# Moving one chunk's loads behind the second weight matrix, its value casts behind a later unit, and small casts between engines, in a one-core attention and feed-forward kernel

## The chip, the cores and the metric

The kernel runs on one core of one Trainium2 chip. The metric is the device time of one execution in microseconds (us). The kernel before takes 230.92 us in the median of 3 runs (230.06 to 231.16). A core has TensorE (PE in the profile; its weight loads are PEld), VectorE (DVE), ScalarE (ACT), GpSimd (POOL) and SyncE (SP), each with its own in-order stream of instructions; DMAs are issued from the streams of SP, ACT and POOL.

## The reference

Inputs are q, k, v of shape (4, 8, 768, 64): 4 batches, 8 heads, 768 positions, 64 values each. Heads with `retr` 1 attend to all earlier positions; the others ("streams") see only the first 4 positions and a window of 64. A feed-forward part follows.

```python
scores = scale * np.matmul(q, k.transpose(0, 1, 3, 2))
...
mask = np.where(retr[0, :, 0, 0, None, None], full_mask, stream_mask)
scores = np.where(mask[None, :, :, :], scores, -1000000000.0)
...
a = np.exp(scores)
a = a / (np.sum(a, axis=-1, keepdims=True) + 1e-09)
return np.matmul(a, v).astype(np.float32)
...
h = x @ w_in
g = h * (1.0 / (1.0 + np.exp(-beta * h)))
return (g @ w_out).astype(np.float32)
```

Here `x` is the attention output as 3072 rows of 512; `w_in` is 512 x 2048 and `w_out` 2048 x 512.

## The kernel before, in words

The work is cut into 8 chunks (a batch and one half of its positions: 384 queries) and each chunk into 4 units (a pair of heads, p = 0 to 3): 32 units, unit u in chunk u // 4. Chunks are computed two batches at a time, first halves before second halves, so the "third chunk" is number 2, units 8 to 11, the second half of batch 0.

For a unit of the first three chunks the steps are these. `load_qk` (L123) brings float32 rows of k and q into staging tiles `s0` (pairs 0 and 1) and `s1` (pairs 2 and 3); `load_v` (L143) brings the values into `vs`, in three 256 KB pieces. With `held`, a tiny memset of the tile by another engine stands ahead of the load, so that the load waits for that engine alone. `cast` (L288) makes bfloat16 copies `qkb` of k and q; `cast_dp(u)` puts k's cast on DVE and leaves q's on POOL, `cast(u)` puts both on POOL. `steps_T` (L363) transposes them on PE and copies them into `KT` and the padded query tiles `QTP` (whose other halves `zero_q` sets to zero). `sinks_of` (L344) copies key blocks of streams into `KO`. `steps_QK` (L442) makes scores and exponentials `es`. `values` (L304) casts the values into `VX` (`cast_v`, L298) and makes the stream copies `VO` on POOL. `steps_PV` (L497) multiplies `es` by `VX` and `VO` into `po`; DVE divides by the sums (`rec`, `x`). `steps_X` (L536) transposes `x` into `xT`; for later units a DMA does it. From chunk 3 on, rows go through POOL's cast DMAs (`load_rows`, L322, twelve 64 KB pieces per chunk: six of k, then six of q, into tiles that `rows` (L249) takes from the same staging pools) and DMA transposes instead.

The feed-forward part has two kinds of step: a "first product" `steps_G1` (L569; four matmuls with `w_in_sb`, a tanh on ACT, a gate on DVE into `gT`), 16 per chunk, and a "second product" `steps_G2` (L592; four matmuls with `w_out_sb`, four such steps to one output tile), 12 per chunk. `next_m` chooses the next one and `ms(n)` takes n of them. `w_in` comes by `load_w_in` (L158), `w_out` by `load_w_out` (L164), both cast during the DMA and issued by POOL.

All five engines' streams are in program order: the order of the calls at L725 to L853 (written out by hand) and of the slots behind it is the order on each engine. `later(delay, fn)` puts a small piece off until the estimated clock has gone on by `delay` ns, which places it in the stream some steps further down. From L1015 the strings `SEQ` give the order of the steps of each group of scores: `1` a first product, `2` a second product, `p` half of a unit's PV; `PVS` names the units.

Names of the steps below: unit 8's T, QK and PV are T(8), QK(8), PV(8); "product 5" is the fifth first product. In the profile a first product is PE L579, a second product PE L623, T is PE L371, QK is PE L486, PV is PE L514, X is PE L546, scores of later groups are PE L961; `cast` is L296, `cast_v` L302, the copies of `sinks_of` L354 and L355, of `values` L315 and L316, `zero_q` L260; the loads are L138 (q, k), L152 (v), L162 (w_in), L166 (w_out), L328 (rows); DMA transposes are L339 (keys, queries) and L530 (x).

Of the kernel before, what the change touches and what calls it, by code (L numbers as in the profile page):

```python
# [17 lines left out]
def kernel(  # L18
# [13 lines left out]
    nc = tc.nc  # L32
# [55 lines left out]
    def later(delay, fn):  # L88

        todo = [fn]  # L90

        def once():
            if todo:
                todo.pop()()
        heapq.heappush(heap, (clock[0] + delay, count[0], once))
        count[0] += 1
        return once
# [5 lines left out]
    def step(s):  # L103
        cost, fn = s
        flush(clock[0])
        clock[0] += cost
        fn()
# [15 lines left out]
    def load_qk(c, g, pairs=1, held=False):  # L123

        b, h2 = chunks[c]
        rows = slice(h2 * HALF, (h2 + 1) * HALF)
        both = stage.tile([128, 2, 2, 2, HT, D], F32, name=f"s{g}")
        for i, (name, src) in enumerate((("k", k), ("q", q))):
            staged[name, c, g] = both[:, i]
            if held:  # L130
                nc.gpsimd.memset(staged[name, c, g][:, 0, 0, 0, 0:1], 0.0)
        n = 2 // pairs
        for i in range(pairs):
            for name, src in (("k", k), ("q", q)):
                h = 2 * g + n * i
                eng = nc.scalar if c == 0 and name == "q" else nc.sync
                for hs in [slice(0, 2)] if n == 1 else [slice(0, 1), slice(1, 2)]:
                    eng.dma_start(  # L138
                        out=staged[name, c, g][:, n * i:n * (i + 1), hs].rearrange("p a h t d -> p (a h) (t d)"),
                        in_=src[b].rearrange("(c a) s d -> a c s d", c=2)[h:h + n, hs, rows, :].rearrange(  # L140
                            "a c (p t) d -> p a c (t d)", t=HT)[:, 0 if n == 1 else slice(0, n), slice(0, 2) if n == 1 else 0])

    def load_v(c, held=False, tiles=range(HT)):  # L143
        b, h2 = chunks[c]
        if tiles[0] == 0:
            staged["v", c] = stage.tile([128, HT, H, D], F32, name="vs")
        vs = staged["v", c]
        if held:
            nc.gpsimd.memset(vs[:, :, 0, 0:1], 0.0)
        for t in tiles:  # L150
            r = h2 * HALF + t * 128
            nc.sync.dma_start(out=vs[:, t], in_=v[b, :, r:r + 128, :].rearrange("h p d -> p h d"))  # L152
# [5 lines left out]
    def load_w_in(i, n=1):  # L158
        f = slice(i * 512, (i + n) * 512)
        view = moe_w_in.rearrange("(c a d) f -> c d a f", c=2, a=MO)  # L160
        for c in range(2):
            nc.gpsimd.dma_start(out=w_in_sb[c * D:(c + 1) * D, :, f], in_=view[c][:, :, f])  # L162

    def load_w_out(i):  # L164
        f = slice(i * 4, (i + 1) * 4)
        nc.gpsimd.dma_start(out=w_out_sb[:, f, :], in_=moe_w_out.rearrange("(fo fi) d -> fi fo d", fi=128)[:, f, :])  # L166
        w_done.add(i)
# [90 lines left out]
    def zero_q(i):  # L258
        for hh in range(2):
            nc.vector.memset(QTB[i][hh][half(1 - hh), :], 0.0)  # L260
# [4 lines left out]
            if streams[p]:  # L265
                eng.memset(VO[b, p][:, :, :, D:D + 1], 1.0)

    for i in range(2):
        zero_q(i)
    negatives()  # L270

# [16 lines left out]
    def cast(u, names=("k", "q"), on=None):  # L288
        b, h2, p = units[u]
        c = u // NPAIR  # L290
        s = st_u.setdefault(u, {})
        if "qkb" not in s:
            s["qkb"] = att.tile([128, 2, HT, 2, D], BF16, name="qkb", bufs=4)
        for name in names:
            copy = on or nc.gpsimd.tensor_copy
            copy(out=s["qkb"][:, "qk".index(name)], in_=staged[name, c, p // 2][:, p % 2].rearrange("p h t d -> p t h d"))  # L296

    def cast_v(u):  # L298
        b, h2, p = units[u]
        c = u // NPAIR  # L300
        copy = nc.scalar.copy if u in (2, 3) else nc.vector.tensor_copy if u < 2 or u in (5, 7) or 8 <= u < 16 else nc.gpsimd.tensor_copy
        copy(out=VX[b % 2, p][:, h2 * HT:(h2 + 1) * HT, :, 0:D], in_=staged["v", c][:, :, p:H:NPAIR, :])  # L302

    def values(u):  # L304

        b, h2, p = units[u]
        ka, kz = (1, 2) if h2 == 0 else (2, 5)
        n = kz - ka
        st_u.setdefault(u, {})["values"] = lambda: None
        cast_v(u)  # L310
        if not streams[p]:
            return
        vx, vo = VX[b % 2, p], VO[b % 2, p]
        h0 = streams[p][0]
        nc.gpsimd.tensor_copy(out=vo[:, ka - 1:kz - 1, :, 0:D], in_=vx[:, ka:kz, h0:2, 0:D])  # L315
        nc.gpsimd.tensor_copy(out=vo[0:n_sink_i, ka - 1:kz - 1, :, 0:D],  # L316
                              in_=vx[0:n_sink_i, 0:1, h0:2, 0:D].to_broadcast([n_sink_i, n, 2 - h0, D]))
# [45 lines left out]
    def steps_T(u):  # L363
        b, h2, p = units[u]
        s = st_u.setdefault(u, {})

        def go():
            tk, tq = tile_t(), tile_t()
            for i, tp in ((1, tk), (0, tq)):
                for t in range(HT):  # L370
                    nc.tensor.transpose(tp[:, t, :], s["qkb"][:, i, t].rearrange("p h d -> p (h d)"), ident)  # L371
            copy = nc.scalar.copy if u == 4 else nc.vector.tensor_copy
            copy(out=KT[b % 2, p][:, h2 * HALF:(h2 + 1) * HALF].rearrange("p (j t) -> p j t", t=HT),
                 in_=tk.rearrange("p t j -> p j t"))
            if u in (3, 7):
                sinks_of(u)
            s["QT"] = QT = QTB[u % 3]
            for hh in range(2):
                copy = nc.vector.tensor_copy if hh else nc.scalar.copy
                copy(out=QT[hh][half(hh), :].rearrange("p (j t) -> p j t", t=HT),  # L380
                     in_=tq[half(hh)].rearrange("p t j -> p j t"))

            if u >= 8:
                s["values"] = later(1500, lambda: values(u))
            if u not in (3, 7):
                s["sinks"] = later(600, lambda: sinks_of(u))
        return [(350, go)]

# [147 lines left out]
    def steps_X(u):  # L536
        b, h2, p = units[u]
        s = st_u.setdefault(u, {})

        def go():  # L540
            c = u // NPAIR
            if c not in xT:
                xT[c] = moe.tile([128, MO, HALF], BF16, name="xT", bufs=3)
            tp = tile_t(u)
            for t in range(HT):
                nc.tensor.transpose(tp[:, t, :], s["x"][:, t].rearrange("p h d -> p (h d)"), ident)  # L546
            copy = nc.scalar.copy if u < 8 and u != 3 else nc.vector.tensor_copy
            copy(out=xT[c][:, p, :], in_=tp.rearrange("p t j -> p (t j)"))
            avail.add((c, p))
            since[c] = clock[0]  # L550
            del st_u[u]
        return [(170, go)]
# [90 lines left out]
    first, second = [], []  # L643
# [63 lines left out]
    def transposes_of(u):  # L707
        step(steps_T(u)[0])

    def run(steps):  # L710
        for x in steps:
            step(x)

    def ms(n):
        for _ in range(n):
            step(next_m())
# [3 lines left out]
    def cast_dp(u):  # L720
        cast(u, "k", dve)
        cast(u, "q")
# [12 lines left out]
    special[0] = Banks(2, 3)  # L735
    transposes_of(1)
    special[0] = None
    zero_q(2)
    st_u[0]["sinks"]()
    step(qk[0])  # L740
    step(qk[1])
    step(qk[2])
    cast_dp(2)
    st_u[1]["sinks"]()
    cast(3)
    qk = steps_QK(1)
# [42 lines left out]
    qk = steps_QK(5)  # L789
    step(qk[0])  # L790
    cast(6)
    load_w_in(1)
    cast(7)
    load_w_in(2, 2)
    ms(1)
    step(qk[1])
# [15 lines left out]
    values(6)  # L812
    values(7)
    run(steps_PV(4))
    load_w_out(0)
    load_w_out(1)
    load_qk(2, 0, held=True)
    load_w_out(2)
    load_w_out(3)
    rows("q", "s1")  # L820
    load_v(2)
    load_qk(2, 1)
    ms(1)
    run(steps_PV(5))
    step(steps_X(4)[0])
    ms(1)
    run(steps_PV(6))
    step(steps_X(5)[0])
    ms(1)
    run(steps_PV(7))  # L830
    step(steps_X(6)[0])
    ms(1)
    step(steps_X(7)[0])
    rows("k", "s0")
    rows3 = load_rows(3)
    load_v(3)
    spare[0] = 1
    ms(8)
    for f in masks_late(1):
        f()  # L840
        ms(2)
    ms(8)
    cast_dp(8)
    for i in range(6):
        rows3[i]()
    for i in range(6, 9):
        later(1000 * (i - 3), rows3[i])
    transposes_of(8)
    for m in second[0:4]:
        step(m[1])  # L850
    done[1] += 4
    spare[0] = 0
    ms(2)  # L853
# [140 lines left out]
    def cycle(k, seq, pvs):  # L994
# [7 lines left out]
        for x in seq:  # L1002
# [10 lines left out]
                special[0] = None  # L1013

    SEQ = ["2p2p2", "X2b", "ap1p11p1p11111pp111pp1122", "22c222112112", "p1p11p1p111pp1112pp2", "b12222121212",  # L1015
           "2p1p1112p1p21pp11pp122", "a111c2221212", "212112121212", "pap11p1p112pp112pp22", "221211211112", "211111112112",
           "2p2p22pcp222"]
    PVS = {0: [11], 1: [11], 2: [14, 12, 13, 15], 4: [18, 16, 17, 19], 6: [22, 20, 21, 23], 9: [26, 24, 25, 27], 12: [30, 28]}

# [79 lines left out]
```

## Time and profile before

| | |
|---|---|
| median of 3 runs | 230.92 us |
| the profiled execution | 232.34 us |
| its span, first to last instruction | 230.6 us |
| ACT busy | 156.1 us (68%) |
| DVE busy | 143.4 us (62%) |
| POOL busy | 101.8 us (44%) |
| mean granted TensorE clock | 0.998 |
| bytes moved by DMA | 31.78 MB |

The profile is of one execution. A row of its timeline gives the start and the length in us, the engine, the source line, the operation with output and inputs, the count of instructions merged into the row and, in brackets, how long the engine had been idle before it and what ended that. SPq, POOLq and ACTq are the instruction streams that issue DMAs. Times within the execution are counted from the span's start.

### The profile page before, as it was taken

To read this page: it belongs to the slowest core of one execution; us is meant where nothing else is said; L and a number is where in the kernel's file an instruction comes from. 1 tells how busy PE (TensorE), PEld (TensorE's weight loads), DVE (VectorE), ACT (ScalarE), POOL (GpSimd) and SP (SyncE) were. 2 spreads that over 40 slices of the span, in tenths; PEclk is the share of its full clock that TensorE was granted. 3 is DMA by queue.
4 is the path that set the end of the run, shared out by engine and by line. 5 is a ranking of instruction groups with operands and counts; after the bars stand their busy time and mean duration, and the time that the engine had idled before them with its cause. 6 is when DMAs were issued, how large, how long until landed. Compare 5 with 4: busy or idle time off the path is not lost.

```text
span 230.6 us, 5261 instructions
## 1 busy us (share of the span) xinstructions
PE 219.7 (95%) x1928; PEld 130.3 (57%) x1928; DVE 143.4 (62%) x356; ACT 156.1 (68%) x306; POOL 101.8 (44%) x226
## 2 busy tenths in 40 slices
PE   6889899997999999999999999999999999999994
PEld 2666666653666566545654555454755556556553
DVE  6775879873768589736946593454781676338700
ACT  3899888944667898657874847684938797128621
POOL 6567740454978998057508695840070000000000
PEclk9999999999999999999999999999999999999999
DMA  6999999999999899956998999952832101211012
GB/s 190 258 241 230 148 187 232 206 196 237 200 191 172 122 167 162 139 125 127 167 186 113 105 207 146 149 130 71 179 59 63 45 3 45 82 47 47 3 45 91
DMA packets 95770, 31.78 MB, mean 138 GB/s; under 512 B 82672, under 2 KB 92288, under 8 KB 95744
## 3 DMA queue, kind: packets, MB, share of 16 engines
q1 hardware_dynamic: 58912, 22.33, 47.2%
q0 software_dynamic: 35424, 8.13, 45.6%
q10 hardware_dynamic: 1408, 0.99, 1.4%
q8 instruction: 15, 0.25, 0.5%
q14 instruction: 11, 0.09, 0.1%
HBM read 27.27 MB, written 6.29 MB: 146 GB/s over the span
## 4 chain that ended last, share of the span: by engine, by line
PE 71%; DMA 11%; DVE 5%; ACT 4%; SPq 3%; POOL 2%; issue 1%; ACTq 0%; DVEq 0%; POOLq 0%
PE tp L623 31%; PE mm L579 26%; DMA vs<-in_v_dram 7%; PE po L514 5%; PE sp L961 5%; SPq L152 3%; DMA w_in_sb<-in_moe_w_in_dram 3%; DMA s<-in_q_dram 2%; PE sp L486 2%; ACT es L490 2%; PE tp L606 2%; DVE es L439 1%; DVE x L519 1%; DVE gT L585 1%; PE tp L371 1%
## 5 line engine op out<-in xcount | busy, mean ns | idle before, releaser
L579 PE MATMUL mm<-xT,w_in_sb 128*128 128x384 bf16 x512 | 92.2, 326 | 0.6 <-DMA w_in_sb<-in_moe_w_in_dram 0.4
L623 PE MATMUL tp<-w_out_sb,gT 128*128 128x512 bf16 x368 | 89.3, 379 | 0.0
L582 ACT ACTIVATE th<-mm,beta_h 128x384 f32<-128x384 f32 x128 | 73.1, 598 | 21.3 <-PE mm L579 15.8
L585 DVE SCALAR_TENSOR_TENSOR gT<-th,mm 128x384 bf16<-128x384 f32 x128 | 67.4, 550 | 29.7 <-ACT th L582 25.4
L579 PEld LDWEIGHTS <-w_in_sb 128*128 128x128 bf16 x512 | 48.0, 98 | 32.2 <-issue 1.1
L623 PEld LDWEIGHTS <-gT 128*128 128x128 bf16 x368 | 33.9, 98 | 33.7 <-issue 0.3
L965 ACT ACTIVATE es<-sp 128x512 bf16<-128x512 f32 (+1 forms) x84 | 39.9, 594 | 4.3 <-PE sp L961 4.3
L630 ACT ACTIVATE osb<-tp 128x512 f32<-128x512 f32 x21 | 12.7, 603 | 31.4 <-PE tp L623 29.8
L490 ACT ACTIVATE es<-sp 128x512 bf16<-128x512 f32 (+1 forms) x44 | 22.5, 559 | 5.5 <-PE sp L486 5.1
L514 PEld LDWEIGHTS <-es 128*128 128x128 bf16 x472 | 20.7, 97 | 8.9 <-issue 1.5
L302 POOL CAST VX<-vs 128x384 bf16<-128x384 f32 x18 | 9.3, 526 | 33.0 <-DMA vs<-in_v_dram 30.5
L439 DVE TENSOR_TENSOR es<-es,Mh 128x512 bf16<-128x512 bf16 (+3 forms) x58 | 20.2, 381 | 4.4 <-ACT es L965 3.7
L328 POOL DMA_DIRECT2D s<-in_q_dram x30 | 22.5, 768 | 0.7 <-issue 0.6
L514 PE MATMUL po<-VX,es 128*128 128x65 bf16 x392 | 22.4, 193 | 0.4 <-DVE x L519 0.4
L328 POOL DMA_DIRECT2D s<-in_k_dram x30 | 22.3, 770 | 0.1
L519 DVE TENSOR_TENSOR x<-po,rec 128x384 bf16<-128x384 f32 x32 | 17.8, 558 | 1.1
L486 PE MATMUL sp<-QTP,KT 128*128 128x128 bf16 (+2 forms) x113 | 15.0, 230 | 0.5 <-DVE QTP L380 0.3
L439 DVE TENSOR_TENSOR es<-es,Mc 128x384 bf16<-128x384 bf16 (+2 forms) x21 | 7.8, 370 | 11.4 <-ACT es L965 10.8
L315 POOL COPY VO<-VX 128x128 bf16<-128x128 bf16 (+3 forms) x24 | 9.5, 395 | 10.6 <-DVE VX L302 9.1
L296 POOL CAST qkb<-s 128x384 bf16<-128x384 f32 x15 | 7.5, 520 | 12.5 <-DMA s<-in_q_dram 12.4
L517 DVE RECIPROCAL rec<-po 128x6 f32<-128x6 f32 x32 | 6.1, 190 | 10.7 <-PE po L514 10.7
L354 POOL COPY KO<-KT 128x128 bf16<-128x128 bf16 (+1 forms) x20 | 8.9, 444 | 8.7 <-DMA KT<-s 5.5
(75 smaller groups left out, 166.2 us busy)
## 6 DMA issues: line engine op xcount, KB each, us to landing
vs<-in_v_dram SPq DMA_DIRECT2D x24, 256.0 KB, 5.9
out_dram<-osb SPq DMA_DIRECT2D x23, 256.0 KB, 2.5
s<-in_k_dram SPq DMA_DIRECT2D x12, 192.0 KB, 5.9
w_out_sb<-in_moe_w_out_dram POOLq DMA_DIRECT2D x4, 512.0 KB, 14.7
s<-in_k_dram POOLq DMA_DIRECT2D x30, 64.0 KB, 5.3
s<-in_q_dram POOLq DMA_DIRECT2D x30, 64.0 KB, 5.2
s<-in_q_dram SPq DMA_DIRECT2D x8, 192.0 KB, 6.7
w_in_sb<-in_moe_w_in_dram POOLq DMA_DIRECT2D x4, 256.0 KB, 5.6
```

Of the source, the lines that this page charges most:

```text
L328: nc.gpsimd.dma_start(out=ROWS[c % 2, name][:, t].rearrange("p (a w) -> p a w", a=NPAIR)[:, :, w:w + D], in_=src[b, hh * NPAIR:(hh + 1) * ...
L439: nc.vector.tensor_mul(e, e, m)
L486: nc.tensor.matmul(sp[:, (i - lo) * 128:(j - lo) * 128], lhs, s["QT"][hh][:, q0 * 128:(q0 + j - i) * 128], start=not added, stop=not added ...
L490: nc.scalar.activation(out=es[:, 0:w], in_=sp[:, 0:w], func=ACTF.Exp, scale=scale)
L514: nc.tensor.matmul(po[:, qi, hh, :], e, val, start=(j == 0), stop=(j == len(lst) - 1))
L519: nc.vector.tensor_mul(x, po[:, :, :, 0:D], rec.to_broadcast([128, HT, 2, D]))
L579: nc.tensor.matmul(hp[:, 0:HALF], w_in_sb[:, mo, fi * 128:(fi + 1) * 128], xT[c][:, mo, :], start=(mo == 0), stop=(mo == MO - 1))
L582: nc.scalar.activation(out=th, in_=hp[:, 0:HALF], func=ACTF.Tanh, scale=beta_h[:, fi:fi + 1])
L585: nc.vector.scalar_tensor_tensor(out=gTs[c][:, fi, :], in0=th, scalar=1.0, in1=hp[:, 0:HALF], op0=ALU.add, op1=ALU.mult)
L623: nc.tensor.matmul(op, gTs[c][:, fi, ns * 128:(ns + 1) * 128], w_out_sb[:, fi, :], start=(fi == 0), stop=(fi == FO - 1))
L630: nc.scalar.activation(out=osb, in_=op, func=ACTF.Copy, scale=0.5)
L965: nc.scalar.activation(out=es[:, 0:w], in_=sp[:, 0:w], func=ACTF.Exp, scale=scale)
```

## The change

It has six parts.

1. The three query tiles are all zeroed at the start by DVE; before, two were, and the third after unit 1's transposes.
2. Unit 2's k is cast by POOL instead of DVE. In `cast_v`, unit 2's values are cast by DVE and unit 3's by POOL; ACT did both.
3. Unit 7's casts (POOL) stand ahead of the issue of w_in's second quarter instead of behind it.
4. The loads behind PV(4): before, two issues of w_out, then s0's memset and loads, two issues of w_out, then v(2) and s1. Now s0's memset and loads, four issues of w_out, then s1 with a memset of its own. v(2) is issued later, behind eight more first products and a memset on DVE; v(3) behind unit 8's transposes and four second products, with a memset on DVE as well.
5. First products 5 to 8 are set anew among PV(5) to PV(7) and X(4) to X(7); the row loads of chunk 3 are spread between the second products; unit 8's values are cast behind unit 9's key copies (`sinks_of(9)`, now at once) rather than 1500 ns of estimated clock after unit 8's transposes.
6. In the seventh group's string of `SEQ`, half a PV goes ahead of the first second product and one first product moves up.

```diff
         if held:
-            nc.gpsimd.memset(vs[:, :, 0, 0:1], 0.0)
+            (nc.gpsimd if held is True else held).memset(vs[:, :, 0, 0:1], 0.0)
...
-    for i in range(2):
+    for i in range(3):
         zero_q(i)
...
-        copy = nc.scalar.copy if u in (2, 3) else nc.vector.tensor_copy if u < 2 or u in (5, 7) or 8 <= u < 16 else nc.gpsimd.tensor_copy
+        copy = nc.vector.tensor_copy if u < 3 or u in (5, 7) or 8 <= u < 16 else nc.gpsimd.tensor_copy
...
+            if u == 9:
+                sinks_of(u)
+                values(8)
             if u >= 8:
-                s["values"] = later(1500, lambda: values(u))
-            if u not in (3, 7):
+                s["values"] = later(1500, lambda: values(u)) if u > 8 else lambda: values(u)
+            if u not in (3, 7, 9):
                 s["sinks"] = later(600, lambda: sinks_of(u))
...
-    zero_q(2)
     st_u[0]["sinks"]()
...
-    cast_dp(2)
+    cast(2)
...
     cast(6)
+    cast(7)
     load_w_in(1)
-    cast(7)
     load_w_in(2, 2)
...
     run(steps_PV(4))
-    load_w_out(0)
-    load_w_out(1)
     load_qk(2, 0, held=True)
-    load_w_out(2)
-    load_w_out(3)
+    for i in range(4):
+        load_w_out(i)
+    load_qk(2, 1, held=True)
     rows("q", "s1")
-    load_v(2)
-    load_qk(2, 1)
-    ms(1)
     run(steps_PV(5))
     step(steps_X(4)[0])
+    run(steps_PV(6))
     ms(1)
-    run(steps_PV(6))
     step(steps_X(5)[0])
+    run(steps_PV(7))
     ms(1)
-    run(steps_PV(7))
     step(steps_X(6)[0])
     ms(1)
     step(steps_X(7)[0])
+    ms(1)
     rows("k", "s0")
     rows3 = load_rows(3)
-    load_v(3)
     spare[0] = 1
     ms(8)
+    load_v(2, held=nc.vector)
...
     cast_dp(8)
-    for i in range(6):
-        rows3[i]()
+    transposes_of(8)
+    for i in range(4):
+        step(second[i][1])
+        for j in range(2 * i, min(2 * i + 2, 6)):
+            rows3[j]()
     for i in range(6, 9):
-        later(1000 * (i - 3), rows3[i])
-    transposes_of(8)
-    for m in second[0:4]:
-        step(m[1])
+        later(1000 * (i - 5), rows3[i])
+    load_v(3, held=nc.vector)
...
-           "2p1p1112p1p21pp11pp122", "a111c2221212", "212112121212", "pap11p1p112pp112pp22", "221211211112", "211111112112",
+           "p2p1111p2p121pp11pp122", "a111c2221212", "212112121212", "pap11p1p112pp112pp22", "221211211112", "211111112112",
```

The instructions are the same in number and kind but for the engines named in part 2 and four small memsets ahead of loads, two on DVE and two on POOL. On POOL the order behind PV(4) becomes: s0's memset, w_out four times, s1's memset, q's cast of unit 8, two row loads, KO copies of unit 8, four row loads, q's casts of units 9 and 10, five row loads, VO copies of unit 8, one row load, VO copies of unit 9. On SP v(2) now stands behind s1, and v(3) behind the first output store.

## Prediction

> **What bounds the kernel now.** I read the page's busy times first, then the windows, to see where TensorE is not full.
>
> ```profile
> PE 219.7 (95%) x1928; PEld 130.3 (57%) x1928; DVE 143.4 (62%) x356; ACT 156.1 (68%) x306; POOL 101.8 (44%) x226
> ```
>
> ```profile
> 10.00:20.00 10.00, 8.68 (x129) 6.94 (x127) 7.62 (x21) 9.70 (x23) 5.55 (x25) 1.00 1.17 258
> 20.00:30.00 10.00, 9.38 (x117) 6.97 (x115) 7.21 (x19) 8.61 (x18) 8.40 (x21) 1.00 1.02 152
> 50.00:60.00 10.00, 8.28 (x51) 4.27 (x50) 3.81 (x11) 3.88 (x8) 4.78 (x9) 1.00 1.36 214
> 60.00:200.00 140.00, 139.25 (x1272) 80.77 (x1270) 89.30 (x224) 99.79 (x197) 69.39 (x131) 1.00 1.04 125
> ```
>
> The columns are the window, its length, then PE, PEld, DVE, ACT and POOL busy. PE is the bound: over 140 us behind 60 it lacks 0.75. The holes stand in front: 1.3 us in 10 to 20, where ACT is the full engine (9.70 of 10), 0.6 in 20 to 30, 1.7 in 50 to 60. What is saved there stays saved, since PE behind it is full. The change leaves PE's matmuls as they are, so it can only close holes or open new ones. The chain that ended last says what made them:
>
> ```profile
> 21.30 6.09 DMA w_in_sb<-in_moe_w_in_dram
> ...
> 38.83 15.66 DMA vs<-in_v_dram
> 54.61 0.37 DVE VX L302
> 55.03 0.36 POOL VO L315
> ...
> 55.79 1.43 POOL s L328 x2
> 57.22 0.52 POOL qkb L296
> ```
>
> Ahead of it stand ACT's value casts (their row is in the next part). So there are three: those casts at 14, w_in's second quarter, landed at 27.39, and v(2), landed at 54.49, behind which POOL makes VO(8), two row loads and only then the q cast of unit 9 that T(9) wants.
>
> **Part by part. The start (parts 1 and 2).**
>
> ```profile
> 3.98 0.20 DVE L219 TENSOR_SCALAR Ns<-Md 128x128 bf16<-128x128 bf16 x1 [0.34 <-POOL Md L193]
> 7.92 1.40 POOL L296 CAST qkb<-s 128x384 bf16<-128x384 f32 x3
> 8.40 0.49 DVE L296 CAST qkb<-s 128x384 bf16<-128x384 f32 x1
> 9.49 0.47 ACT L380 COPY QTP<-tp 64x384 bf16<-64x384 bf16 x1 [0.62 <-PE tp L371]
> 13.92 0.92 ACT L302 CAST VX<-vs 128x384 bf16<-128x384 f32 x2
> 13.98 0.29 POOL L316 COPY VO<-VX 4x128 bf16<-4x128 bf16 x1
> 14.73 0.92 ACT L296 CAST qkb<-s 128x384 bf16<-128x384 f32 x2
> 14.89 0.30 POOL L315 COPY VO<-VX 128x128 bf16<-128x128 bf16 x1 [0.62 <-ACT VX L302]
> ```
>
> The third tile's memsets (some 0.5 us) move in front of the masks; DVE waits 0.34 for POOL there, so 0.0 to 0.15 is left: I take 0, and without that wait it would be 0.5. Unit 2's two casts on POOL end at 7.92 + 2 x 0.47 = 8.86, no later than DVE's single one (8.89), but k is ready half a microsecond sooner, so half of T(2)'s 0.5 us lies ahead: ACT's copy starts some 0.2 sooner. ACT then loses its 0.92 of value casts, and unit 4's casts start 1.1 sooner. Not all of it reaches PE: POOL now casts unit 3's values itself (0.5) behind its copies that end at 14.27, so VO(3) starts at 14.27 - 0.2 + 0.5 = 14.57 instead of 14.89. That 0.3, and ACT being free for it, is PE's gain. I take **0.35**; bounds 0 (POOL's five casts cancel it) and 1.1 (ACT's whole time).
>
> POOL's work isn't always equally fast: the cast below took 0.69, where those at 7.92 took 0.47 each.
>
> ```profile
> 62.60 0.69 POOL L296 CAST qkb<-s 128x384 bf16<-128x384 f32 x1
> ```
>
> The slow one ran while DVE multiplied masks. If DVE's value cast of unit 2 held up POOL's VO copies in the same way, by no more than its own length (0.37, as in the chain at 54.61), this part would bring nothing: a rival below. The Trainium skill ("SBUF — State Buffer", section "Who interferes with whom") states such a rule against this part: VectorE's casts in a two-port mode, and its operations with two SBUF inputs, take a port pair that GpSimd shares, and the later of the two blocks. The row above agrees for the mask products; for casts no row here decides.
>
> **Products 5 to 8 (parts 3 and 5).**
>
> ```profile
> 21.91 0.97 POOL L296 CAST qkb<-s 128x384 bf16<-128x384 f32 x2
> 27.35 0.56 DVE L519 TENSOR_TENSOR x<-po,rec 128x384 bf16<-128x384 f32 x1
> 27.52 0.81 PE L579 MATMUL mm<-xT,w_in_sb 128*128 128x384 bf16 x4 [0.44 <-DMA w_in_sb<-in_moe_w_in_dram]
> 31.85 0.17 PEld L546 LDWEIGHTS <-x 128*128 128x128 bf16 x3 [0.48 <-DVE x L519]
> 32.84 0.32 PE L579 MATMUL mm<-xT,w_in_sb 128*128 128x384 bf16 x1 [0.16 <-ACT xT L548]
> ```
>
> Three small stalls: 0.44 for w_in, about 0.3 on X(7), whose weight load had waited 0.48, and 0.16 for the last copy of xT: 0.9. The new order closes the last two: no gates stand between the divisions on DVE, and product 8 covers X(7)'s copy. w_in's issue goes behind 0.97 of casts, against 0.35 gained: it lands 0.6 later, near 28.0. But product 5 comes later too: PE would end PV(4) near 26.7, does PV(5), and X(4) waits for x(4), done at 27.91 - 0.35 = 27.55; X(4) and PV(6) take 0.55, product 5 is at 28.1. So w_in's 0.44 is replaced by 0.45 on x(4), and the other two stay saved: **0.45**. Bounds: -0.5 (w_in lands the full 0.97 later) and 0.9. T(8) comes 0.8 sooner.
>
> **The loads (part 4) and unit 9.**
>
> ```profile
> 43.51 0.50 POOL L296 CAST qkb<-s 128x384 bf16<-128x384 f32 x1 [12.09 <-DMA s<-in_q_dram]
> 48.28 5.34 PE L623 MATMUL tp<-w_out_sb,gT 128*128 128x512 bf16 x24
> 51.65 5.77 SPq L152 DMA_DIRECT2D vs<-in_v_dram  x3
> 56.57 0.55 DVE L296 CAST qkb<-s 128x384 bf16<-128x384 f32 x1 [1.14 <-DMA s<-in_k_dram]
> 57.79 0.34 PE L371 MATMUL tp<-idb,qkb 128*128 128x128 bf16 x3 [1.72 <-POOL qkb L296]
> 61.62 0.28 PE L514 MATMUL po<-VX,es 128*128 128x65 bf16 x4
> ```
>
> The hole at 57.79 is 1.72 of PE. Now neither DVE nor POOL waits for v(2) ahead of unit 9. POOL's order after KO(8) (near 48.1, or 49 as before) is four row loads of 0.75 and q's cast: ready at 52 to 53, while T(9) would come at 55. The hole is closed: **1.7** (0.9 if POOL's row loads take its place, 1.9 at most).
>
> Who is late next? v(2) and s1, 768 KB each, have changed places. s1's k landed at 56.5 (the wait of 56.57), its q by 57.2, where POOL's second cast began; so v(2) lands there at the latest by order alone, and sooner as s0's and s1's loads start earlier. It is wanted by DVE behind KO(9), which is at 59.3 now and near 57 then, and by PV(8), at 61.62 now and 59 then. No wait if it lands by 57; I take **-0.2**, bounds 0 and -3.6, the rival below.
>
> w_out is the other one:
>
> ```profile
> L166 POOL DMA_DIRECT2D w_out_sb<-in_moe_w_out_dram x4: 755/760/770, 28.4 to 30.7; - x4
> ...
> DMA to landing us min/median/max: 9.9/14.7/18.5
> ```
>
> Its last piece lands at 30.65 + 18.5 = 49.15, and the fourth second product, which reads it, stands at 48.28 + 3 x 0.87 = 50.9: 1.75 of cover, 0.95 when PE is 0.8 sooner. s0's loads begin 1.5 us earlier beside it and may take half of the transfers' time then, 0.75; s1 in place of v(2) is not priced by any row. I take **-0.1**, bounds 0 and -0.8.
>
> Behind 60 only one transfer is close:
>
> ```profile
> 64.70 4.01 SPq L339 DMA_TRANSPOSE QTD<-s  x3
> 74.89 0.99 PE L961 MATMUL sp<-QTD,KT 64*128 64x384 bf16 x16
> ```
>
> The query transposes of chunk 3 leave SP by 68.7 and PE wants them at 74.9, at 72.2 after a gain of 2.7. SP's stream ahead of them follows the output stores, thus PE, and chunk 3's row loads end sooner on POOL. I take **-0.1**, bounds 0 and -1.
>
> **The seventh group (part 6).**
>
> ```profile
> 133.77 0.28 PE L514 MATMUL po<-VX,es 128*128 128x65 bf16 x4 [0.21 <-DVE x L519]
> 136.65 0.34 PE L514 MATMUL po<-VX,es 128*128 128x65 bf16 x6 [0.23 <-DVE x L519]
> ```
>
> PE waits twice for a division before it may reuse the `po` bank. In the changed order the first division stands three mask products sooner on DVE (7 of them take 2.55, so 1.1), and PE has a product more in between. The second still stands behind four gates. I take **0.3**, bounds 0 and 0.45.
>
> The sum: 0.35 + 0.45 + 1.7 - 0.2 - 0.1 - 0.1 + 0.3 = 2.4. The profiled execution is 232.34, 1.42 over the median of the runs and 1.74 over its own span; what lies around the span is not touched. 232.34 - 2.4 = 229.94 there, **228.5** in the median.
>
> **The rivals.** *The early gains don't arrive, only T(9)'s does.* POOL is the new queue in front: two casts more, two ahead of w_in. For it: POOL is busy 8.40 of 10 in 20 to 30. Against it: it idles in 10 to 20 (5.55). Then parts 1 to 3 give 0, and 1.7 - 0.4 + 0.3 = 1.6 is left: 229.3.
>
> *POOL is held up beside DVE's cast.* Then the start's 0.35 goes to the 0.37 that unit 2's cast takes on DVE: 228.9. For it speaks the cast of 0.69; against it, that POOL's copies at 13.98 and 14.89 (0.29, 0.30) need only meet DVE's cast once. The rule of the Trainium skill named above ("SBUF — State Buffer") would give this case.
>
> *v(2) becomes the late one, and it is slower.* DVE's stream stops at unit 8's value cast, and behind it stand unit 9's values and unit 8's masks, then PV(8) and all of PE. It decides from the point where v(2) lands later than 57. For it: SP's issues are held back already (v(3)'s three take 5.77), and if v(2) moves only once s1 has landed (57.2), at the pace of those issues (two thirds of 5.77, or all of it), it lands at 61.1 to 63.0. From 61.5, with two casts (0.7) and two masks (an estimate, 0.7 as well), PV(8) comes at 62.9 instead of 61.62: the front's gains are gone and 1.3 is lost, less 0.3 in the seventh group: 231.9. Against it: by bytes it only takes s1's place.
>
> *The hole at T(9) comes back as another wait.* POOL issues six row loads around unit 9's cast, 0.75 each; if KO(8) holds the first four until 51 and s1 is late for unit 10, T(9) or T(10) waits about 1.2: 228.5 + 1.2 = 229.7, no change that can be told.
>
> **How the numbers follow.** Forecast 0.55; T(9) alone 0.17; POOL held up 0.05; the hole comes back 0.11; v(2) late 0.12. A measurement of this kernel can tell about 0.5%, 1.15 us: faster means below 229.77, slower above 232.07. The first three are nearly always below: 0.74. The hole's return, the rest of those three and a fourth of v(2)'s case are within: 0.17. The rest of v(2)'s case is above: 0.09. The best bounds together would take 0.75 + 0.45 + 0.2 + 0.4 + 0.15 = 1.95 more off; they hardly fall together, and I keep 1.7: 226.8. Upward the range covers all cases but most of v(2)'s: 231.2, where v(2) would cost 2.7 more than I take.
>
> **What would show it.** Right: no PE wait on POOL's cast at T(9); ACT's idle 0.62 at 9.49 down to 0.4; unit 4's casts on ACT near 13.7; the wait of 0.44 for w_in gone and one on x(4) in its place; T(8) near 47.2; PV(8) near 59; at 133 one wait of DVE's division fewer. Wrong: DVE idle before unit 8's value cast with v(2) as its releaser, a PE wait on w_out near 50, or a wait on DMA transposes at the first scores of chunk 3. T(8) at 48 would show that the start gave nothing.

## The result and the profile after

The changed kernel takes **229.54 us** in the median of 7 runs (229.31 to 229.70). The kernel before, run beside it, takes 230.66 (7 runs, 230.06 to 232.27). The ratio is 0.994 with a 95% interval of 0.9914 to 0.9966: faster by 0.6%, and 1.0 more than the 228.5 that was forecast. The profiled executions differ by more: 232.34 before, 229.70 after, 2.64. In the sessions below before's median was 230.72 to 230.90 each time, so times of different sessions are set beside each other. A run that the measurement marks as disturbed is left out of the counts and the medians.

The page of the changed kernel, its busy times and the shares of its chain of waits:

```profile
PE 218.5 (96%) x1908; PEld 130.7 (57%) x1928; DVE 143.0 (63%) x358; ACT 155.0 (68%) x304; POOL 102.2 (45%) x230
PE 84%; DVE 6%; ACT 3%; POOL 2%; DMA 2%; issue 2%; SPq 0%; POOLq 0%; ACTq 0%
```

20 matmul records of L626 are missing (348 of 368 on the page), which alone can make PE's busy time look smaller than before's (218.5 beside 219.7). The lines behind L383 have moved by 3: a second product is L626 now, T is still L371. The windows show where the time came from (columns as before: PE, PEld, DVE, ACT, POOL):

```profile
10.00:20.00 10.00, 8.63 (x131) 6.98 (x129) 7.98 (x22) 9.08 (x22) 6.04 (x27) 1.00 1.15 256
20.00:30.00 10.00, 9.25 (x122) 7.00 (x121) 7.51 (x20) 8.10 (x18) 8.16 (x20) 1.00 1.01 167
50.00:60.00 10.00, 9.95 (x72) 5.49 (x72) 5.00 (x16) 5.46 (x11) 8.69 (x15) 1.00 1.64 213
```

The hole in 50 to 60 is gone: PE 8.28 before, 9.95 now. In 10 to 20 ScalarE has lost its value casts (9.70 to 9.08), and PE has gained nothing by it. The timeline of the changed kernel at the places that the prediction named, in order of time (start, duration, then the idle time before it and who ended it):

```profile
5.56 0.51 ACT L296 CAST qkb<-s 128x384 bf16<-128x384 f32 x1 [1.15 <-DMA s<-in_k_dram]
...
9.55 0.47 ACT L380 COPY QTP<-tp 64x384 bf16<-64x384 bf16 x1 [0.60 <-PE tp L371]
...
12.73 0.94 DVE L302 CAST VX<-vs 128x384 bf16<-128x384 f32 x3
13.15 0.29 POOL L315 COPY VO<-VX 128x64 bf16<-128x64 bf16 x1 [0.45 <-DVE VX L302]
13.51 0.24 POOL L316 COPY VO<-VX 4x64 bf16<-4x64 bf16 x1
...
13.98 0.92 ACT L296 CAST qkb<-s 128x384 bf16<-128x384 f32 x2
14.29 0.50 POOL L302 CAST VX<-vs 128x384 bf16<-128x384 f32 x1
14.86 0.30 POOL L315 COPY VO<-VX 128x128 bf16<-128x128 bf16 x1
15.29 0.48 ACT L551 COPY xT<-tp 128x384 bf16<-128x384 bf16 x1 [0.39 <-PE tp L549]
...
26.67 0.30 POOL L315 COPY VO<-VX 128x128 bf16<-128x128 bf16 x1 [1.25 <-DVE VX L302]
27.03 0.46 POOL L316 COPY VO<-VX 4x128 bf16<-4x128 bf16 x1
27.54 0.19 PE L517 MATMUL po<-VO,es 128*128 128x65 bf16 x1 [0.32 <-POOL VO L316]
28.09 0.34 PE L549 MATMUL tp<-idb,x 128*128 128x128 bf16 x3 [0.27 <-DVE x L522]
...
47.64 0.50 PE L371 MATMUL tp<-idb,qkb 128*128 128x128 bf16 x6
47.98 5.34 PE L626 MATMUL tp<-w_out_sb,gT 128*128 128x512 bf16 x23
...
55.43 0.50 PE L371 MATMUL tp<-idb,qkb 128*128 128x128 bf16 x6
...
57.82 0.63 DVE L302 CAST VX<-vs 128x384 bf16<-128x384 f32 x2
59.41 0.28 PE L517 MATMUL po<-VX,es 128*128 128x65 bf16 x4
...
134.01 0.34 PE L517 MATMUL po<-VX,es 128*128 128x65 bf16 x6 [0.17 <-DVE x L522]
```

T(9) at 55.43 waits for nobody, and VectorE's casts of units 8 and 9 at 57.82 find v(2) landed. PV(8) comes at 59.41, near the 59 that was named, and at 133 one of the two waits on a division is gone. In front the signs came late or not at all: T(8) comes at 47.64 and not near 47.2, ScalarE's idle time at 9.55 is 0.60 where 0.4 was forecast, ScalarE's casts for unit 4 start at 13.98, not 13.7 (14.73 before), and VO(3) comes at 14.86, where it came at 14.89: GpSimd's own cast (14.29, 0.50) stands where it used to wait for ScalarE.

One execution each can't price parts of 0.3. The marks below are starts of rows of PE's timeline in all 14 profiled executions of this study: the first scores of unit 4, T(8), the first scores of the group that begins near 77 (L961 with `QTD` and `KT`), and the span.

| kernel | unit 4's scores | T(8) | scores near 77 | span |
|---|---|---|---|---|
| before | 17.56 | 47.95 | 78.97 | 230.6 |
| before again | 17.48 | 47.70 | 79.63 | 231.0 |
| loads alone | 17.50 | 47.96 | 77.08 | 228.4 |
| loads alone again | 17.57 | 48.06 | 77.19 | 228.7 |
| seventh group alone | 17.59 | 47.90 | 77.03 | 228.5 |
| start and products alone | 17.42 | 47.38 | 76.50 | 227.8 |
| changed | 17.51 | 47.64 | 76.76 | 228.0 |
| changed again | 17.16 | 47.12 | 76.25 | 227.1 |
| changed, old start | 17.47 | 47.56 | 76.68 | 227.7 |
| changed, old products | 17.30 | 48.46 | 77.58 | 228.8 |
| changed, old loads | 17.29 | 47.63 | 76.87 | 227.9 |
| changed, old seventh group | 17.36 | 47.71 | 76.83 | 228.2 |
| changed, one more load | 17.29 | 47.29 | 77.57 | 228.4 |
| changed, earlier cast | 17.32 | 48.27 | 77.40 | 228.3 |

### The profile page after: what moved, and what is told of

It reads as the page before. It is cut to its first block, busy times and chain, and to the rows that moved or that the text cites. A ratio compares the mean times of both kernels' runs of the same rounds, so it can differ in the third digit from the quotient of the medians.

```text
span 228.0 us, 5247 instructions
## 1 busy us (share of the span) xinstructions
PE 218.5 (96%) x1908; PEld 130.7 (57%) x1928; DVE 143.0 (63%) x358; ACT 155.0 (68%) x304; POOL 102.2 (45%) x230
## 4 chain that ended last, share of the span: by engine, by line
PE 84%; DVE 6%; ACT 3%; POOL 2%; DMA 2%; issue 2%; SPq 0%; POOLq 0%; ACTq 0%
PE mm L582 34%; PE tp L626 34%; PE po L517 6%; PE sp L961 5%; PE sp L489 2%; DMA s<-in_k_dram 2%; PE tp L609 2%; DVE gT L588 1%; PE tp L371 1%; ACT es L965 1%; DVE QTP L380 1%; DVE es L442 1%; ACT QTP L380 1%; PE tp L549 1%; DVE x L522 1%
## 5 line engine op out<-in xcount | busy, mean ns | idle before, releaser
L626 PE MATMUL tp<-w_out_sb,gT 128*128 128x512 bf16 x348 | 86.7, 379 | 1.1 <-issue 0.2
L626 PEld LDWEIGHTS <-gT 128*128 128x128 bf16 x368 | 33.9, 98 | 33.7 <-issue 0.3
L633 ACT ACTIVATE osb<-tp 128x512 f32<-128x512 f32 x21 | 12.7, 604 | 31.4 <-PE tp L626 29.8
L442 DVE TENSOR_TENSOR es<-es,Mh 128x512 bf16<-128x512 bf16 (+3 forms) x58 | 20.7, 390 | 4.8 <-ACT es L965 4.2
L442 DVE TENSOR_TENSOR es<-es,Mc 128x384 bf16<-128x384 bf16 (+2 forms) x21 | 7.1, 341 | 11.4 <-ACT es L965 10.8
L961 PE MATMUL sp<-QTD,KT 64*128 64x128 bf16 (+2 forms) x199 | 11.8, 232 | 0.0
```

The source lines that it names most:

```text
L442: nc.vector.tensor_mul(e, e, m)
L626: nc.tensor.matmul(op, gTs[c][:, fi, ns * 128:(ns + 1) * 128], w_out_sb[:, fi, :], start=(fi == 0), stop=(fi == FO - 1))
L961: nc.tensor.matmul(sp[:, a * 128:z * 128], lhs[half(h)], st_u[u]["QT"][half(h), q0 * 128:(q0 + z - a) * 128], start=True, stop=True)
```

## The experiments

The theory after the result: the wait at T(9) is a race of v(2)'s landing against VectorE's stream, and it has another length in each execution; the 1.72 of the profiled one was not the usual one. The rival: it is the same in each, and the early parts of the change lost what it gave.

**Before again.** No edit.

> The kernel before, unchanged. Theory: TensorE's wait of 1.72 at T(9) is v(2)'s landing against VectorE's stream, and differs between executions; the profiled execution of before (span 230.6) had a long one, and most have 0.3 to 0.6. Then a second profiled execution has a span near 229 (1.4 less) and a wait at T(9) below 1.0, v(2) landing before 54, with the rest of the program as it was. Rival: the wait is 1.5 to 1.9 in every execution, and the first profiled execution lost its 1.4 elsewhere: then the second one shows the same wait and a difference in front of it or behind it. Timed: the same as before, within 0.3%.

Measured: 230.79 in the median (12 runs, 230.44 to 233.19), ratio to before 0.9992 (0.9961 to 1.0024). The theory expected a short wait in this profiled execution; it was another long one, 232.66. Its timeline:

```profile
55.27 0.36 DVE L302 CAST VX<-vs 128x384 bf16<-128x384 f32 x1 [4.81 <-DMA vs<-in_v_dram]
55.69 0.35 POOL L315 COPY VO<-VX 128x192 bf16<-128x192 bf16 x1 [6.25 <-DVE VX L302]
...
58.44 0.34 PE L371 MATMUL tp<-idb,qkb 128*128 128x128 bf16 x3 [1.96 <-POOL qkb L296]
```

v(2) let VectorE go at 55.27 here and at 54.61 in the first profiled execution: 0.66 later, and the wait is 1.96 beside 1.72, with another one of 0.50 ahead of it for k's cast. So the length goes with the landing in these two. That there are short ones is shown by the next run.

**The seventh group alone.**

```diff
-           "2p1p1112p1p21pp11pp122", ...
+           "p2p1111p2p121pp11pp122", ...
```

> Before with the seventh group's order alone. Theory: 0.4 off (the two traces differ by 0.43 from there on), ratio 0.998; the first of TensorE's two waits on VectorE's division is gone, the second stays near 0.3. Rival: the wait only moves to a later product or PV: ratio 1.000, and TensorE stands where it did at 140.

Measured: 230.23 (7 runs, 229.67 to 231.24), ratio 0.9951 (0.9926 to 0.9976): 0.66 off in the median, more than the theory's 0.4. Its loads are those of before, and this is what its profiled execution (span 228.5) shows at T(9):

```profile
52.20 0.36 DVE L302 CAST VX<-vs 128x384 bf16<-128x384 f32 x1 [1.54 <-DMA vs<-in_v_dram]
...
54.80 0.54 POOL L296 CAST qkb<-s 128x384 bf16<-128x384 f32 x1
55.69 0.50 PE L371 MATMUL tp<-idb,qkb 128*128 128x128 bf16 x6
```

v(2) landed 2.4 to 3.1 sooner than in the two executions above, from loads issued at the same point of the program, and T(9) doesn't wait at all. That settles the theory against its rival: the same loads give a wait of 0, 1.7 or 2 and more. By the landing times in the traces, the last of v(2)'s three pieces lands at 50.9, 51.8 and 52.1 in the three executions with the old loads that don't wait at T(9) (two of them are of kernels further down), and at 54.5 and 55.2 in the two that do.

**Part 4 alone, the loads.** The change's diff from `load_w_out(0)` to `load_v(3)` and in `steps_T`, with the order of X and products of before.

> Before with the loads of chunk 2 (v(2) behind s1, w_out's issues together), unit 8's value cast behind unit 9's copies and the row loads between second products: part 4 alone. Theory: it closes the wait at T(9), which is 0.3 to 0.6 in most runs: 0.4 off the median, ratio 0.998, and the spread of the runs (2.2 us in before) falls below 0.6. Rival, the prediction's term: 1.7 less 0.4 for w_out, v(2) and the transposes, so 1.3 off, ratio 0.9945.

Measured: 230.80 (eleven runs, 230.02 to 233.08), ratio 0.9989 (0.996 to 1.0017): neither the theory's 0.4 nor the forecast's 1.3, and the spread stayed. The profiled execution, one of its quick ones (230.16), has no wait at T(9).

**Part 4 alone, again.** The same kernel once more, for a slower execution.

> Part 4 alone once more, because half of its runs stood 0.7 to 3.5 above its lowest and its one profiled execution was among the quick ones. The changed kernel, with the same loads, had no such run in 19. Theory: its slow runs are executions in which the last piece of w_out lands after 50.9 (49.73 in the quick one, 1.2 of room); a slow profiled execution shows a wait on w_out near 51. Rival: they wait for w_in at 27.5, which the changed kernel's order of products hides behind PV(5) and X(4); then the wait of 0.66 there is longer and nothing waits at 51. Third: v(2) ahead of unit 8's value cast. If the profiled execution is a quick one again, this stays open; the lowest run should then be within 0.2 of before's lowest.

Measured: 230.79 (12 runs, 230.15 to 231.82), ratio 0.9987 (0.9958 to 1.0016). The lowest run is 0.41 above before's (229.74), where 0.2 was expected. The profiled execution was quick again (230.40), without a wait at T(9) or on w_out. What the slower runs of this kernel wait for stays open.

**The start and products 5 to 8 alone**, with the loads and the seventh group of before.

> Before with the start (third zeroed tile at the start, unit 2's and 3's casts as changed), w_in's issue behind both casts and the order of products 5 to 8: the loads and the seventh group stay as before. Theory: the start brings 0, products 5 to 8 bring 0.3 at T(8), and the wait at T(9), which ends with v(2)'s landing, takes that back or most of it: 0 to 0.3 off, ratio 0.999 to 1.000. Rival, the prediction's terms: 0.35 + 0.45 = 0.8 off at T(8), and with the loads issued as much sooner it stays: ratio 0.9965.

Measured: 229.81 (ten runs: nine from 229.25 to 230.48, one at 231.80), ratio 0.9953 (0.9924 to 0.9983): 1.1 off, not the theory's 0 to 0.3; the prediction's 0.8 is nearer. Its T(8) comes at 47.38, and v(2) was early again in the profiled execution, so that nothing was taken back at T(9).

**The changed kernel again**, beside three kernels that differ from it in one thing.

> The changed kernel again, on the chip and beside the runs of before that the other kernels of this call get. Theory: before's runs have a floor near 229.8 and a tail up to 232.9, because TensorE waits at T(9) by as much as the transfers of 30 to 57 us are late in that execution; the change lowers the floor by 0.4 to 0.5 (products 5 to 8) and takes most of the tail away: median 229.6, most runs within 0.5 of the lowest. Rival: the tail only moves to w_out, which in the changed kernel lands 0.75 ahead of the product that reads it (49.86 against 50.6): then part of the runs stand 0.7 to 2 above the lowest, as in part 4 alone, and the median is 230.0 to 230.5.

Measured: 229.39 (12 runs, 228.84 to 229.87), ratio 0.9931 (0.9903 to 0.996), beside 230.72 for before. All 12 lie within 1.03; in 19 runs of the changed kernel there is none that stands apart. The tail is gone, as the theory had it, and the rival's 230.0 or more did not come. The theory's sizes are off: the lowest run is 0.85 below before's (229.69), not 0.4 to 0.5, and only five of the 12 lie within 0.5 of the lowest.

The first of the three has the old start again:

```diff
-    for i in range(3):
+    for i in range(2):
         zero_q(i)
...
-        copy = nc.vector.tensor_copy if u < 3 or u in (5, 7) or 8 <= u < 16 else nc.gpsimd.tensor_copy
+        copy = nc.scalar.copy if u in (2, 3) else nc.vector.tensor_copy if u < 2 or u in (5, 7) or 8 <= u < 16 else nc.gpsimd.tensor_copy
...
+    zero_q(2)
     st_u[0]["sinks"]()
...
-    cast(2)
+    cast_dp(2)
```

> The changed kernel with the start as before (third zeroed tile behind T(1), unit 2's k on VectorE, values of units 2 and 3 on ScalarE). Theory: the start brings nothing, since GpSimd's chain of unit 3's values takes the place of ScalarE's casts: lowest run and median as the changed kernel's within 0.15, T(4) within 0.1 of it. Rival, the prediction's term: 0.35 slower.

Measured: 229.95 (12 runs, 229.38 to 230.67), 0.56 above the changed kernel. So the start is not worth nothing. Its size by the marks: unit 4's first scores come at 17.47 to 17.59 in the six profiled executions with the old start (mean 17.53) and at 17.16 to 17.51 in the seven with the new one that have no other edit in front (mean 17.33): **0.20**. The new start's size hangs on the first loads. ScalarE's cast of unit 1's k is begun when its load lets it; counted from there, unit 4's scores come 12.24 to 12.29 later with the old start and 11.95 to 12.10 with the new one in the same executions, **0.27** apart. Two rows, the first from the changed kernel run again, the others from this one with the old start:

```profile
8.36 0.79 PE L371 MATMUL tp<-idb,qkb 128*128 128x128 bf16 x6 [0.46 <-POOL qkb L296]
```

```profile
8.31 0.49 DVE L296 CAST qkb<-s 128x384 bf16<-128x384 f32 x1
8.85 0.51 PE L371 MATMUL tp<-idb,qkb 128*128 128x128 bf16 x6 [1.00 <-DVE qkb L296]
```

T(2) comes 0.49 sooner, as the prediction had it for k. The changed kernel's first profiled execution, on which "the start gave nothing" rests, is the latest of the seven (17.51); there ScalarE got unit 1's k only at 5.56 (the first row of the timeline above), where in the second it began that cast at 5.15.

The second has the old loads again; unit 8's value cast, the row loads and v(3) go back with them, in hunks not shown:

```diff
     run(steps_PV(4))
+    load_w_out(0)
+    load_w_out(1)
     load_qk(2, 0, held=True)
-    for i in range(4):
-        load_w_out(i)
-    load_qk(2, 1, held=True)
+    load_w_out(2)
+    load_w_out(3)
     rows("q", "s1")
+    load_v(2)
+    load_qk(2, 1)
...
     ms(8)
-    load_v(2, held=nc.vector)
```

> The changed kernel with chunk 2's loads, unit 8's value cast and the row loads as before (so: start, products 5 to 8 and seventh group alone). Theory: the lowest run as the changed kernel's within 0.2, but with before's tail, since T(9) still follows v(2): a third of the runs 0.7 or more above the lowest, median 0.3 to 0.6 above the changed kernel's. Rival: the loads bring nothing at all, and the medians agree within 0.2.

Measured: 229.74 (eleven runs: eight from 229.21 to 230.31, three from 231.79 to 232.51), ratio to before 0.9967 (0.9923 to 1.0011). The lowest run is 0.37 above that of the changed kernel, the median 0.35, and the runs fall in two heaps whose middles are 2.3 apart (229.6 and 231.9), between the 1.9 and 2.8 that T(9) cost in the two executions that waited there (below). The profiled execution was one of the quick ones. With the rest of the change in place, the new loads take the upper heap away; that the upper heap waits at T(9) is the likeliest reading, but it is not shown: no such run was profiled.

The third has one more load, read by nothing, behind w_out's first piece:

```diff
+    more = wpool.tile([128, 2, d_model], BF16, name="more")
     for i in range(4):
         load_w_out(i)
+        if i == 0:
+            nc.gpsimd.dma_start(out=more, in_=moe_w_out.rearrange("(fo fi) d -> fi fo d", fi=128)[:, 0:2, :])
```

> The changed kernel with a fifth transfer, half the size of a piece of w_out and read by nothing, behind w_out's first piece: every later transfer of 38 to 57 us lands some 1.9 later (half of the 3.7 to 4.7 between two pieces), as in an execution with slow transfers. Theory: w_out is then the late one, its last piece at 51.8 against 50.6: TensorE waits 1.2 there and for nothing else, since v(2), at 56.5, is still ahead of the 57.8 at which VectorE wants it: 1.2 slower. Rival: v(2) is the late one, VectorE waits for it ahead of unit 8's value cast and PV(8) comes 1 or more late; w_out costs nothing. Third: neither, the room is larger than the trace shows: 0 to 0.3.

Measured: 230.45 (10 runs, 229.91 to 231.28), 1.06 above the changed kernel. The timeline of PE, and VectorE's casts behind it:

```profile
47.62 2.75 PE L626 MATMUL tp<-w_out_sb,gT 128*128 128x512 bf16 x11
51.38 2.75 PE L626 MATMUL tp<-w_out_sb,gT 128*128 128x512 bf16 x12 [1.00 <-DMA w_out_sb<-in_moe_w_out_dram]
...
58.63 0.63 DVE L302 CAST VX<-vs 128x384 bf16<-128x384 f32 x2
```

The wait is on w_out and nowhere else. T(8) to the scores near 77 takes 30.28 instead of 29.12: 1.16 by the marks, where 1.2 was expected. The casts at 58.63 have no wait for v(2). So with this load w_out is the transfer that is late next; the prediction looked to v(2). The load stands ahead of three of w_out's own pieces on GpSimd, so it presses on w_out more than on v(2); the room that each has without it is given below.

**The seventh group undone, and an earlier cast.** The first is the changed kernel with the string above put back.

> The changed kernel with the seventh group's order as before. Theory: only one of the two waits on VectorE's division comes in most executions (134 to 137: one of 0.30 to 0.39 in three of five profiles, two in the first), and the new order takes it away: 0.2 slower than the changed kernel. Rival, the prediction's term: both waits come, 0.3 to 0.45 slower. Third: another wait stands in for it and the time is the same within 0.1.

Measured: 230.01 (12 runs, 229.54 to 231.34), 0.62 above the changed kernel. PE in its profiled execution:

```profile
134.20 0.34 PE L517 MATMUL po<-VX,es 128*128 128x65 bf16 x6 [0.23 <-DVE x L522]
```

From the scores near 77 to the end of the span the old order takes 151.3 to 151.6 (mean of six 151.42), the new one 150.8 to 151.5 (mean of eight 151.07): **0.35**. That is the prediction's term, although in five of the six old ones only one of its two waits is there. All of it falls between the scores that begin 48.95 behind those near 77 and the next group's: up to there all 14 executions agree within 0.02, the next group begins another 12.8 to 13.1 later with the old order and 12.4 to 12.7 with the new one.

```diff
     st_u[0]["sinks"]()
+    cast(2)
     step(qk[0])
...
-    cast(2)
     st_u[1]["sinks"]()
```

> The changed kernel with unit 2's casts ahead of unit 1's KO copies on GpSimd (its rows have landed by 6.8, and GpSimd begins the cast at 7.8, behind copies that wait for KT(1)). Theory: T(2) comes 0.4 sooner (8.0 instead of 8.4), ScalarE's copy of it too, and half of that or more reaches T(4): 0.2 to 0.4 faster than the changed kernel. Rival: the first value casts (12.4) or ScalarE's exponentials set T(4), and it brings nothing.

Measured: 229.40 (12 runs, 228.69 to 231.16), ratio 0.994 (0.9906 to 0.9974); the changed kernel's in its own session is 0.9931. Five runs lie below 228.95, where the changed kernel has one in 19, but four lie above 230. The profiled execution is one of these (230.05):

```profile
7.41 0.50 POOL L296 CAST qkb<-s 128x384 bf16<-128x384 f32 x1 [0.86 <-DMA s<-in_k_dram]
7.97 0.34 PE L371 MATMUL tp<-idb,qkb 128*128 128x128 bf16 x3
...
20.45 0.81 PE L582 MATMUL mm<-xT,w_in_sb 128*128 128x384 bf16 x4 [0.83 <-DMA w_in_sb<-in_moe_w_in_dram]
```

T(2) starts at 7.97, as expected, and then the first product waits 0.83 for w_in's first quarter. Unit 4's scores come at 17.32, at the mean of the other kernels with the new start: what T(2) gained did not reach them, as the rival had it. It is no gain that can be told; issuing w_in sooner along with it was not tried.

**The products' order undone.** The changed kernel with w_in's issue, PV(5) to PV(7), X(4) to X(7) and products 5 to 8 as before.

> The changed kernel with the order of w_in's issue, PV(5) to PV(7), X(4) to X(7) and products 5 to 8 as before. In the profiles so far T(8) comes 30.37 behind the first scores of unit 4 with the old order (mean of five) and 30.12 with the new one (mean of seven). Theory: the order is worth these 0.25 in a quick execution, and more where w_in is late: the old order wants its second quarter at 27.5, the new one at 28.1 behind PV(5) and X(4). That is why part 4 alone kept a tail of slow runs and the changed kernel has none. Then the lowest run is 0.2 to 0.4 above the changed kernel's (228.84 to 229.31), a third of the runs stand 0.7 or more above the lowest, and the median is near 230.1. Rival: the order has nothing to do with the tail; the runs lie within 0.6 of the lowest but for one or two, and the median is 229.65 to 229.8 (0.25 on top of the changed kernel's).

Measured: 230.02 (12 runs, 229.34 to 231.22), ratio 0.9951 (0.9918 to 0.9984): 0.63 above the changed kernel, six runs 0.7 or more above the lowest. The theory's median came, but its cause did not show. The profiled execution, a slower one (230.52), has its wait elsewhere:

```profile
26.36 0.70 POOL L302 CAST VX<-vs 128x384 bf16<-128x384 f32 x1 [2.56 <-DMA vs<-in_v_dram]
27.12 0.43 PE L517 MATMUL po<-VX,es 128*128 128x65 bf16 x9 [0.62 <-POOL VX L302]
27.97 0.81 PE L582 MATMUL mm<-xT,w_in_sb 128*128 128x384 bf16 x4
```

PV(4) waits for unit 4's value cast, which waits for v(1); product 5 at 27.97 doesn't wait for w_in. By the marks, from unit 4's scores to T(8), the old order takes 30.22 to 30.49 in the five other executions that have it, the new one 29.96 to 30.35 in seven (means 30.37 and 30.12): **0.25**. This execution (31.16) and the one with the earlier cast (30.96), each with the long wait shown, are left out. Whether the new order also keeps late transfers off PE, as the medians suggest, is not settled.

## Why the forecast was right in sign and too low

By its own steps:

- **The hole at T(9): the mechanism right, the size taken from one execution.** This is the step that failed. The term was 1.7, the wait of the profiled execution, and it was subtracted from a median. T(8) to the scores near 77 takes 29.1 with no hole; before it took 31.02 and 31.93 in its two profiled executions, and 29.1 to 29.2 in the three others that have before's loads. So the hole was 1.9, 2.8, 0, 0 and 0.1. The prediction had the hint in hand: the profiled execution stood 1.42 above the median, and it let that excess stand unchanged through the change ("232.34 - 2.4 = 229.94 there, 228.5 in the median"), when the hole of 1.9 by the marks is more than all of it. For the profiled executions the sum is near, 2.4 forecast and 2.64 measured, but in part by luck: start and products gave 0.31 there instead of 0.80, while the hole gave 1.9 instead of 1.7, the seventh group 0.43 instead of 0.3, and none of the 0.4 taken off for transfers came.
- **The sum for an ordinary run.** The marks without a hole give 17.53 + 30.37 + 29.12 + 151.42 = 228.44 before and 17.33 + 30.12 + 29.12 + 151.07 = 227.64 after. With the 1.7 between span and time that is 230.1 and 229.3. The changed kernel's medians, 229.54 and 229.39, stand within 0.2 of it. Before's, 230.66 to 230.90, stand 0.5 to 0.8 higher; late transfers in the middle run are the likely reason, which no profile of such a run shows. So the three small terms make 0.80 of the gain, and 0.3 to 0.5 is left for the hole (1.12 and 1.33 measured, less 0.80). That is a remainder and no measurement of it.
- **The start**: 0.35 forecast, 0.20 by the marks (0.0 to 0.4 by execution), 0.27 where the first loads are counted out. Its working was right: VO(3) was forecast 0.3 sooner, and counted from ScalarE's cast of unit 1's k it comes 0.27 sooner in the mean. That VO(3) stands at 14.86 beside 14.89 in the first pair is the late load of that execution: in the changed kernel run again it stands at 14.50. Most of ScalarE's freed 0.9 turned into idle time (0.39 at 15.29 for X's transposes, and 0.28 behind it), and the prediction had allowed for that.
- **Products 5 to 8**: 0.45 forecast, 0.25 by the marks. The wait for w_in gave way to one on x(4) (0.27 at 28.09), as forecast. The other wait, 0.32 for VO(5) at 27.54, was not seen coming. GpSimd's queue did not make it: GpSimd stood idle for 1.25 until VectorE had cast unit 5's values (26.67), and the second copy, for which PV(5) waits, took 0.46 (27.03). Before, the same rows stood at 26.55 (after 1.33 of idle time) and 26.91, but product 5 ahead of PV(5) covered them.
- **w_out -0.1, v(2) -0.2, transposes -0.1**: none showed in the changed kernel's two profiled executions. The order of danger was the other way round: the row 47.98 gives w_out's first read by the fourth product at 47.98 + 12 x 0.22 = 50.6, its last piece lands 19.1 behind its issue at 30.8, at 49.9 (view below), and that is 0.7 of room. v(2)'s last piece lands at 54.6 in that execution, and VectorE asks for it at 57.8: 3.2 of room. With one more load w_out cost 1.16 while v(2) cost nothing.

```profile
L166 POOL DMA_DIRECT2D w_out_sb<-in_moe_w_out_dram x4: 759/768/780, 28.6 to 30.8; - x4
...
DMA to landing us min/median/max: 9.1/14.6/19.1
```

- **The seventh group**: 0.3 forecast, 0.35 by the marks.

Of the rivals, "the early gains don't arrive, only T(9)'s does" gave 229.3 and "the hole comes back as another wait" 229.7, both nearer to the time than the forecast and both for the wrong reason: start and products do arrive (0.45 together by the marks, 1.1 off in the median when they are made alone), no other wait stands at T(9) or T(10), and it is the hole that is smaller in the middle run. "v(2) becomes the late one" didn't come either.

GpSimd beside VectorE's cast: from GpSimd's first VO copy to VO(3) takes 1.70 or 1.71 in all eight executions with the new start and 1.80 in the six with the old, so that rival is out here. The rule behind it (the Trainium skill, "SBUF — State Buffer", section "Who interferes with whom") has instances all the same. The copy at 27.03 began 0.05 behind a cast on VectorE and took 0.46; this copy takes 0.45 or 0.46 in 13 of the 14 executions, and the other 99 copies of its form take 0.29. It stood in before's profile too (26.91), where the prediction found no row that decides for casts. GpSimd's cast at 26.36 in the last experiment began within 0.02 of one on VectorE and took 0.70, where those alone take 0.50. The copy lost 0.17 and the cast 0.20, less than the 0.31 and 0.34 for which they lay beside VectorE's cast: these rows show a part of the time lost, and not the whole.

What doesn't add up: taking one part from the changed kernel costs 0.35 to 0.63 in the median each, 2.2 together, more than the 1.1 to 1.3 that all four bring; and the loads alone bring 0.1 or less. Medians of 12 runs are known to some 0.3% (0.7 us) here, and late transfers that one part leaves to the next may do the rest. It is left open.

## What to carry to other kernels

A wait that a DMA ends need not be a fixed cost; here it was next to nothing in three executions and 1.9 and 2.8 in two: look at how far the profiled execution stands above the median of the runs, and suspect such a wait of being that excess before it is entered in a sum against the median. Price small parts by marks, the distance between two fixed instructions of the bound engine over several profiled executions, and not by medians of kernels that carry a tail. When a load is moved, compare the slack of every transfer that shares its window, and not only of the one that moved.

## What was not expected of the hardware

The same loads, issued at the same point of kernels that are alike up to there, landed up to 3 us apart from one execution to the next: v(2) let VectorE go at 54.61, 55.27 and 52.20, in executions whose T(8) agree within 0.25. The granted clock between 50 and 60 is 1.00 in all three, so it is not the engines' pace. The lateness is older than the wait: between 28 and 32, ahead of v(2)'s issue, DMA moved 158 GB/s in the two executions that waited, and 175, 186 and 198 in the three others with the old loads. Why is open. The same showed in front: the first product waited 0.83 for w_in at 20.45 in one execution, and PV(4) 0.62 for v(1) at 27.12 in another. The changed kernel's 19 runs lie between 228.84 and 229.87 all the same. In the nine profiled executions with the new loads v(2)'s last piece lands anywhere from 53.5 to 56.3, but VectorE asks for it only at 57.3 to 58.6, and it waits in none of them.
